# A hand-made order for the first batch, and TensorE in program order, in a kernel of attention and two feed-forward networks

## The chip, the cores and the metric

The kernel runs on one core of one Trainium2 chip. The metric is the device time of one execution, in microseconds (us); the median of three runs of the kernel before is 913.62 us. A core has five engines that run side by side: TensorE (PE) for matmuls, with its weight loads shown apart (PEld), VectorE (DVE), ScalarE (ACT), GpSimd (POOL), and SyncE (SP), which here issues nearly all DMA transfers. Each engine takes its instructions in a fixed order, made when the program is built, and they wait for one another by semaphores.

## The reference

```python
def _attn_ref(q, k, v):                       # (4, 8, 576, 64) each
    ...
    q_d = q.reshape(B, H, Sd, factor, D).mean(axis=3)      # pooled by 4: Sd = 144, also k_d, v_d
    out_up = np.repeat(sm_attn(q_d, k_d, v_d), factor, axis=2)
    mask = np.abs(pos[:, None] - pos[None, :]) < factor    # window of 7 keys
    ...
    return out_up + out_local
def _moe_ref(x, w1, w2, w3, w_out):            # 2304 tokens, 512 -> 768 -> 512
    h = np.maximum(np.maximum(x @ w1, x @ w2), x @ w3)
    return h @ w_out
def _moe2_ref(x, w_in, w_out):                 # 512 -> 2048 -> 512
    h = x @ w_in
    return np.maximum(0.01 * h, h) @ w_out
```

The attention's output, 4 batches of 576 rows with 8 heads of 64, is the 2304 x 512 input of the first network, whose output is that of the second.

## The kernel before, in words

**Tiling.** The 2304 tokens are eight *units* of 288, two to a batch (u = 0 to 7). For each unit the first network runs 18 groups L1 (six blocks m, three weights e) and four groups L2. A number is held as a high and a low part in a 22 bit format, so a product takes three matmuls: L1 is 12 matmuls of 128x128 by 288 columns, L2 is 18. The input parts are xh and xl, the hidden ones hh and hl. A group is called a *slot*: 22 slots a unit, `PU`. The second network (L3, L4) runs over chunks of 512 tokens when all units are done.

**Weights.** They arrive as 64 bit numbers. `split_weight` makes the two parts: two ScalarE instructions, two on VectorE (line 157 and 160), one on ScalarE, one subtraction on GpSimd or VectorE (line 166). The first network has 24 weight tiles (18 wA and 6 wO), named W1.

**Attention.** Pooled attention runs per batch and group of two heads (h = 0 to 3): load, pooling sums of q and k (line 478), scores on TensorE (492), softmax, transposes (516), product with v (531), result `up`. The windowed attention of batch 0 (u = 0 and 1) runs on TensorE: a band mask is added by a matmul (376), then scores (379), exponentials, transposes (417), product (426), and the sum with `up` gives x, xh and xl. That of batches 1 to 3 (units 2 to 7), the *local attention*, runs on the other engines with 128 rows of partitions: products of q and k on GpSimd (line 247), sums on VectorE (257) or ScalarE (260), softmax, products with v and sums on VectorE (291, 298) into O. `emit_T` then transposes O (nine transposes, line 573), adds `up`, and makes xh (ScalarE, 601) and xl (VectorE, 602) of the unit.

**What sets the order.** Only SP's order is that of the program (`manual_schedule(engines={SP})`). For the other four a scheduler with a model of the instructions' times picks the order, out of the order in which the program is written. There, the steps of batch 0's four heads come first, one step apart (`items`), with the weight conversions between them; then unit 0's slots, with the pieces for u = 1 in the first nine (`U1`), pieces of the local attention spread over each unit's slots (`loc_p`), the pooled steps of the later batches at given slots (`acts`), and `emit_T(u + 1)` in the second L2 slot. `keep_warm` puts 20 and 40 matmuls without use on TensorE. SBUF tiles of the first batch (`late_tile`) lie in the places of the last 12 weight tiles.

Of the kernel before, what the change touches and what calls it, by code (L numbers as in the profile page):

```python
# [23 lines left out]
G = 32  # L24
# [19 lines left out]
U1 = 9  # L44
AHEAD = 14
NA = 8
NWARM = (20, 40)
# [5 lines left out]
def local_global_attention_moe_kernel(  # L53
# [61 lines left out]
    ps_mm = p1.enter_context(tc.tile_pool(name="ps_mm", bufs=4, space=PSUM))  # L115
    ps_at = p1.enter_context(tc.tile_pool(name="ps_at", bufs=2, space=PSUM))

    ps_early = tc.alloc_tile_pool(name="ps_early", bufs=2, space=PSUM)
# [4 lines left out]
    for edge in (None, "first", "last"):  # L123
        bd = sup.tile([QB, KB], BF16, name=f"band_{edge}")
        P.memset(bd, 0.0)
        conds = [(1, -1, 0), (-1, 1, KB - QB)]
        if edge == "first":
            conds.append((1, 0, -(FAC - 1)))
        if edge == "last":
            conds.append((-1, 0, KB - FAC))  # L130
        for step, cm, base in conds:
            P.affine_select(
                out=bd, in_=bd, pattern=[[step, KB]], base=base, channel_multiplier=cm,
                compare_op=ALU.is_ge, fill=-(2.0**33),
            )
        bands.append(bd)

# [10 lines left out]
    def split_weight(raw, stage, lo_engine):  # L148
# [7 lines left out]
        A.activation(out=l3, in_=low16, func=AF.Copy, scale=2.0**-13, bias=-0.5 + 2.0**-14)  # L156
        V.scalar_tensor_tensor(  # L157
# [184 lines left out]
    def pl_load(what, h):  # L342
# [25 lines left out]
    def pl_scores(u, h, hh):  # L368
        qr, kr = pl[h, "q"], pl[h, "k"]
        pst = ps_early.tile([QB, 512], F32, tag="early", name="ps_ls")  # L370
        ps = pst[:, : NBLK * KB].rearrange("p (n k) -> p n k", n=NBLK)
        st = pst[:, NBLK * KB :]
        rows = slice(64 * hh, 64 * hh + 64)
        for j in range(NBLK):
            band = bands[1 if u == 0 and j == 0 else 2 if u == 1 and j == NBLK - 1 else 0]
            T.matmul(out=ps[:, j], lhsT=ident_b, rhs=band, start=True, stop=False)
            s0 = u * NCOL + j * QB
            qs, ks = slice(s0, s0 + QB), slice(s0, s0 + KB)
            T.matmul(out=ps[:, j], lhsT=qr[rows, qs], rhs=kr[rows, ks], start=False, stop=True)  # L379
        nm = sup.tile([QB, NBLK], F32, tag="plnm", bufs=4, name="plnm")  # L380
        if hh == 0:
            pl[u, h, "sum"] = sup.tile([QB, 2, NBLK], F32, tag="plsm", bufs=4, name="plsm")
        sm = pl[u, h, "sum"][:, hh]
        V.tensor_reduce(out=st[:, :NBLK], in_=ps, axis=AX.X, op=ALU.max, negate=True)
        V.tensor_scalar(out=nm, in0=st[:, :NBLK], scalar1=SCALE, scalar2=None, op0=ALU.mult)
        if hh == 0:
            if u == 0:
                pl[u, h, "e"] = late_tile([QB, 2, NBLK, KB], "ple")
            else:
                pl[u, h, "e"] = sup.tile([QB, 2, NBLK, KB], F32, tag="ple", bufs=2, name="ple")  # L390
        e = pl[u, h, "e"][:, hh]
        for j in range(NBLK):
            A.activation(
                out=e[:, j], in_=ps[:, j], func=AF.Exp, scale=SCALE,
                bias=nm[:, j : j + 1], accum_out=sm[:, j : j + 1],
            )
        if hh == 1:
            e, sm = pl[u, h, "e"], pl.pop((u, h, "sum"))
            sp = st[:, NBLK : 3 * NBLK].rearrange("p (x n) -> p x n", x=2)
            V.tensor_scalar(out=sp, in0=sm, scalar1=1e-9, scalar2=None, op0=ALU.add)  # L400
            V.reciprocal(out=sm, in_=sp)
            for x in range(2):
                (P if u == 0 else V).tensor_tensor(
                    out=e[:, x], in0=e[:, x], in1=sm[:, x].unsqueeze(2).to_broadcast((QB, NBLK, KB)), op=ALU.mult
                )

    def pl_aT(u, h):
# [4 lines left out]
        for n, (j0, j1) in enumerate(((0, 2), (2, 3))):  # L412
            pool, tag = (ps_mm, "mm") if u == n == 0 else (ps_at, "at")
            pt = pool.tile([KB, j1 - j0, 2, QB], F32, tag=tag, name="ps_lt")
            for j in range(j0, j1):
                for hh in range(2):
                    T.transpose(out=pt[:, j - j0, hh], in_=pl[u, h, "e"][:, hh, j], identity=ident[:QB, :QB])
# [13 lines left out]
    def pl_x(u, h):  # L431
# [38 lines left out]
    def ds_pool_qk(b, h):  # L470
# [478 lines left out]
```

## Time and profile before

| | us |
|---|---|
| median of three runs | 913.62 (913.1 to 914.03) |
| the profiled execution | 914.8, its span 913.0 |
| TensorE, weight loads busy | 860.4 and 754.7 |
| VectorE, ScalarE, GpSimd busy | 526.8, 412.8, 247.7 |
| mean granted TensorE clock | 0.932 of full speed |

The page shows the span in 40 slices: TensorE is 90% busy or more from the middle of the span on, and the clock is down in the first tenth and, now and then, up to 0.45 of it. All of GpSimd's work and most of VectorE's lies in the first 0.55 of the span. Durations overlap a little: an instruction can start before the one ahead of it on its engine has ended, so a sum of means is somewhat above the time that a row of them takes. The row of a matmul with fp32 operands counts two records for one matmul.

### The profile page before, as it was taken

Reading aid. Unit: us, or ns where it says so; the run is one execution under the profiler, and the core shown is the slowest. Engines: PE = TensorE matmul, PEld = TensorE weight load, DVE = VectorE, ACT = ScalarE, POOL = GpSimd, SP = SyncE. Lnnn points to the kernel's source line nnn. Section 1 sums busy time; section 2 is a strip of 40 time slices with the busy share of each in tenths; the row PEclk is TensorE's granted clock in tenths of the full one; section 3 lists DMA queues with packets and bytes.
Section 4 is the critical chain, followed back from the end, with each engine's and each line's share of the span. In section 5 each row is a group of like instructions: output and inputs, shape, how many; then the busy total and the mean of one; then the engine's idle time right before and its main releaser. Section 6 shows DMA issues by size and latency. Waiting matters only on the chain.

```text
span 913.0 us, 13518 instructions
## 1 busy us (share of the span) xinstructions
PE 860.4 (94%) x4912; PEld 754.7 (83%) x4914; DVE 526.8 (58%) x919; ACT 412.8 (45%) x1537; POOL 247.7 (27%) x195
## 2 busy tenths in 40 slices
PE   8799988997989989799999999999999999999995
PEld 4478888996978979699999888888887888788894
DVE  3587888887968696777475699242223322322321
ACT  2664754655647456572274687232223222222221
POOL 3553539764755566350111000000000000000000
PEclk9555979897999999799999999999999999999998
DMA  8700624442423133112062920020003000200000
GB/s 219 269 1 24 254 72 147 167 135 70 136 95 122 33 122 111 48 46 73 1 235 105 355 120 1 0 93 1 1 0 93 1 1 2 68 1 1 19 29 23
DMA packets 30132, 75.13 MB, mean 82 GB/s; under 512 B 3267, under 2 KB 8691, under 8 KB 30067
## 3 DMA queue, kind: packets, MB, share of 16 engines
q1 hardware_dynamic: 25459, 69.56, 22.8%
q10 hardware_dynamic: 4608, 4.72, 1.5%
q8 instruction: 38, 0.62, 0.3%
q14 instruction: 27, 0.22, 0.1%
HBM read 64.83 MB, written 9.44 MB: 81 GB/s over the span
## 4 chain that ended last, share of the span: by engine, by line
PE 74%; DVE 12%; DMA 7%; issue 2%; ACT 2%; SPq 1%; POOL 1%; ACTq 0%; POOLq 0%; DVEq 0%
PE ps_h L614 21%; PE acc L717 20%; PE ps_g L693 20%; PE ps_o L644 5%; DMA raw<-x2d 2%; PE ps_up L531 2%; DVE O L298 2%; DVE xl L602 2%; DMA wA<-in_wa_dram 2%; PE ps_ls L379 2%; PE ps_lo L426 1%; DMA sv<-in_vW_dram 1%; DVE wl L157 1%; DVE wy L160 1%; DVE x L594 1%
## 5 line engine op out<-in xcount | busy, mean ns | idle before, releaser
L614 PE MATMUL ps_h<-xh,wA 128*128 128x288 f32 x1152 | 204.5, 311 | 6.3 <-ACT xh L601 3.1
L614 PEld LDWEIGHTS ps_h<-xh,wA 128*128 128x128 f32 x1152 | 177.9, 201 | 9.2 <-ACT xh L601 3.3
L717 PE MATMUL acc<-w2o,gh 128*128 128x512 f32 x576 | 178.2, 391 | 0.9 <-ACT gh L704 0.9
L693 PE MATMUL ps_g<-x2h,w2i 128*128 128x512 f32 (+1 forms) x640 | 158.9, 370 | 0.0
L701 DVE TENSOR_TENSOR g<-g,ps_g 128x512 f32<-128x512 f32 (+1 forms) x80 | 50.7, 634 | 184.0 <-ACT g L700 183.9
L693 PEld LDWEIGHTS ps_g<-x2h,w2i 128*128 128x128 f32 x640 | 114.6, 188 | 22.9
L700 ACT ACTIVATE g<-ps_g 128x512 f32<-128x512 f32 (+1 forms) x80 | 44.3, 553 | 185.2 <-PE ps_g L693 185.1
L614 PE MATMUL ps_h<-xl,wA 128*128 128x288 f32 x576 | 116.5, 308 | 10.7 <-DVE xl L602 10.7
L717 PEld LDWEIGHTS acc<-w2o,gh 128*128 128x128 f32 x576 | 106.8, 188 | 23.7 <-ACT gh L704 1.8
L247 POOL TENSOR_TENSOR qkprod<-lq,lk 128x1344 f32<-128x1344 f32 x36 | 112.0, 3120 | 42.6 <-DVE O L298 25.6
L717 PE MATMUL acc<-w2o,gl 128*128 128x512 f32 x288 | 112.2, 391 | 0.1
L614 PEld LDWEIGHTS ps_h<-xl,wA 128*128 128x128 f32 x576 | 93.2, 199 | 12.9 <-DVE xl L602 11.9
L260 ACT ACTIVATE qkprod<-qkprod 128x64 f32<-128x64 f32 x364 | 87.6, 245 | 24.2 <-POOL qkprod L247 23.8
L693 PE MATMUL ps_g<-x2l,w2i 128*128 128x512 f32 (+1 forms) x320 | 79.6, 370 | 0.0
L644 PE MATMUL ps_o<-hh,wO 128*128 128x288 f32 x384 | 77.4, 298 | 0.0
L705 DVE TENSOR_TENSOR gl<-g,gh 128x512 fp32r<-128x512 f32 (+1 forms) x80 | 51.0, 638 | 39.6 <-ACT gh L704 35.1
L260 ACT ACTIVATION_READ_ACCUMULATOR qkprod<-qkprod 128x1 f32 x364 | 69.6, 191 | 0.0
L704 ACT ACTIVATE gh<-g 128x512 fp32r<-128x512 f32 (+1 forms) x80 | 47.1, 588 | 42.6 <-DVE g L701 42.2
L693 PEld LDWEIGHTS ps_g<-x2l,w2i 128*128 128x128 f32 x320 | 56.8, 188 | 10.9
L635 POOL TENSOR_TENSOR hl<-hm,hh 128x288 fp32r<-128x288 f32 x48 | 40.9, 854 | 88.3 <-ACT hh L634 84.7
L717 PEld LDWEIGHTS acc<-w2o,gl 128*128 128x128 f32 x288 | 54.1, 188 | 12.6 <-DVE gl L705 0.9
L631 DVE TENSOR_TENSOR hm<-hm,ps_h 128x288 f32<-128x288 f32 x96 | 42.3, 445 | 32.8 <-PE ps_h L614 26.9
(124 smaller groups left out, 1216.2 us busy)
## 6 DMA issues: line engine op xcount, KB each, us to landing
wA<-in_wa_dram SPq DMA_DIRECT2D x18, 512.0 KB
w2i<-in_w_in_dram SPq DMA_DIRECT2D x16, 512.0 KB
w2o<-in_w_out_dram SPq DMA_DIRECT2D x16, 512.0 KB
lv<-in_vL_dram SPq DMA_DIRECT2D x12, 480.0 KB
lk<-in_k_dram SPq DMA_DIRECT2D x11, 480.0 KB
dsrawv<-in_vP_dram SPq DMA_DIRECT2D x16, 288.0 KB
x2d<-ev ACTq DMA_DIRECT2D x32, 144.0 KB
raw<-x2d SPq DMA_DIRECT2D x16, 256.0 KB
```

The costliest lines, as they stand in the source:

```text
L247: P.tensor_tensor(out=pr, in0=in0, in1=in1, op=ALU.mult)
L260: A.activation(out=pr[:, r, j], in_=pr[:, r, j], func=AF.Copy, accum_out=sc[:, r, j : j + 1])
L614: T.matmul(out=ps, lhsT=wA[m, e][wi][:, kk * 128 : kk * 128 + 128], rhs=xx[:, kk] if u < PEU else xx[:, :, kk, :], start=n == 0, stop=n == ...
L631: V.tensor_tensor(out=t, in0=t, in1=ps, op=ALU.max)
L635: P.tensor_tensor(out=hl[:, m], in0=t, in1=hh[:, m].bitcast(F32), op=ALU.subtract)
L644: T.matmul(out=ps, lhsT=wO[m][wi][:, os_], rhs=xx[:, m], start=n == 0, stop=n == 3 * M1 - 1)
L693: T.matmul(out=ps, lhsT=w2i[m][wi][:, kk * 128 : kk * 128 + 128], rhs=xx[:, kk, :n], start=j == 0, stop=j == 3 * KC - 1,)
L700: A.activation(out=g, in_=ps, func=AF.Copy, scale=0.01)
L701: V.tensor_tensor(out=g, in0=g, in1=ps, op=ALU.max)
L704: A.activation(out=gh, in_=g, func=AF.Copy)
L705: V.tensor_tensor(out=gl, in0=g, in1=gh.bitcast(F32), op=ALU.subtract)
L717: T.matmul(out=accs[c, t], lhsT=a[:, ts], rhs=w, start=m == 0 and j == 0, stop=m == M2 - 1 and j == 2)
```

## The change

**Orders.** Batch 0 is written in the order of a table, `ORDER`: a letter is a step, a digit the head (or, for x y z u, the weight tile: the four steps of a conversion). In this part all five engines take the program's order. From unit 0 on, SP and TensorE do; the other three are scheduled as before. The pieces of u = 1 move to slots 3h, 3h + 4 and 3h + 5; the local attention begins at slot 15 (`U1`) and its pieces are spread to end at the slots in `DONE`; `emit_T` stands at the slots in `TURN`, and the steps of pooled attention at `DS0` plus `DSOFF`. Eight weight tiles are converted in the first part, the other 16 in unit 0's first 15 slots.

**Warm-up.** `fill` puts 20 matmuls at the start, 8 ahead of step O0, and one or two ahead of the steps B, C, O, M, N and P of each head.

**Engines.** GpSimd takes the pooling of q and k for batches 1 to 3 (two adds in place of a sum of VectorE), xl in `emit_T`, and the normalisation for u = 1. In W1's conversion one intermediate (`wl`) lies in PSUM, and GpSimd does all the low parts. The band mask is added for three blocks in one matmul. PSUM has one pool of seven banks for the first part. O has two buffers.

**Loads.** The tiles of v are padded with zero rows: 102 to 112 partitions and 72 to 80.

```diff
-U1 = 9
-AHEAD = 14
+U1 = 15
-NWARM = (20, 40)
+ORDER = (
+    "C0 A0 A1 L0 B0 D0 A2 C1 E0 L1 F0 B1 H0 G0 D1 I0 x0 C2 J0 L2 F1 E1 y0 K0 G1 D2 O0 L3 H1 E2 J1 M0 "
...
+FILL = {"B": 1, "C": 1, "O": 2, "M": 2, "N": 2, "P": 2}
+FILL0 = 20
+FILL1 = 8
+DONE = {2: 39, 3: 59, 4: 79, 5: 100, 6: 121, 7: 142}
+TURN = {2: 41, 3: 62, 4: 82, 5: 103, 6: 124, 7: 145}
+DS0 = {1: (15, 18, 21, 24), 2: (27, 38, 49, 60), 3: (68, 79, 90, 101)}
+DSOFF = {1: (0, 2, 5, 8, 6, 7, 11, 13), 2: (0, 5, 6, 9, 10, 11, 16, 20), 3: (0, 5, 6, 9, 10, 11, 16, 20)}
...
+    def fill(what, t, n=None):
+        for _ in range(FILL[what] if n is None else n):
+            T.matmul(out=t, lhsT=warm[:, :128], rhs=warm, start=True, stop=True)
...
-        l3 = stage.tile([128, 512], I32, tag="wy", bufs=4, name="wl3")
+        l3 = (stage.tile([128, 512], I32, tag="wy", bufs=4, name="wl3") if ps is None else ps()).bitcast(I32)
...
+    def pl_C(u, h):
...
+        if u == 0:
+            fill("C", pst[0])
+        for t in pst:
+            T.matmul(
+                out=t[:QB, :n], lhsT=ident_b, rhs=bands[u].rearrange("p n k -> p (n k)"), start=True, stop=False
+            )
         for j in range(NBLK):
...
+            for hh in range(2):
+                rows = slice(64 * hh, 64 * hh + 64)
+                T.matmul(
+                    out=pst[hh][:QB, j * KB : j * KB + KB], lhsT=qr[rows, qs], rhs=kr[rows, ks],
+                    start=False, stop=j == NBLK - 1,
+                )
...
-            V.tensor_reduce(out=t[:, j], in_=dst.pop((b, h, w)), axis=AX.X, op=ALU.add)
+            if b == 0:
+                V.tensor_reduce(out=t[:, j], in_=raw, axis=AX.X, op=ALU.add)
+            else:
+                P.tensor_tensor(out=raw[:, :, 0:2], in0=raw[:, :, 0:2], in1=raw[:, :, 2:4], op=ALU.add)
+                P.tensor_tensor(out=t[:, j], in0=raw[:, :, 0], in1=raw[:, :, 1], op=ALU.add)
...
-            V.tensor_tensor(
+            P.tensor_tensor(
                 out=xl[:, g0:g1].rearrange("p r a g -> p (r a g)"), in0=x32f, in1=xhf.bitcast(F32), op=ALU.subtract
             )
...
-    with tc.manual_schedule(engines={mybir.EngineType.SP}):
+    with tc.manual_schedule(engines={ET.SP, ET.PE, ET.DVE, ET.Activation, ET.Pool}):
...
+        for w in ORDER.split():
+            n = int(w[1])
+            if w[0] in "xyzu":
+                conv_step(W1[n])
+            elif w[0] == "L":
+                pl_pool_v(n)
+            else:
+                if w == "O0":
+                    fill("", scratch(0, "", "warm_ps"), FILL1)
+                steps[w[0]](0, n)
...
+    with tc.manual_schedule(engines={ET.SP, ET.PE}):
...
+        for u in range(PEU, NU):
+            at(TURN[u], lambda u=u: emit_T(u))
```

How the instructions stand on TensorE at the first scores of batch 0, before (`ps_sc` are the pooled scores, `ps_ls` the windowed ones of the two halves, `warm` the matmuls without use):

```order
L784 MATMUL warm_ps_212<-warm_210 128x512
L492 MATMUL ps_sc_237<-dsqke_233 72x144 x2
L492 MATMUL ps_sc_247<-dsqke_233 72x144 x2
L376 LDWEIGHTS ident_b_94
L376 MATMUL ps_ls_260<-band_first_122,ident_b_94 96x102
...
L379 MATMUL ps_ls_260<-skr_148,sqr_146 96x102
L376 LDWEIGHTS ident_b_94
L376 MATMUL ps_ls_260<-band_None_114,ident_b_94 96x102
```

and now:

```order
L166 MATMUL ps_ls_220<-warm_130 128x512
L421 LDWEIGHTS ident_b_94
L421 MATMUL ps_ls_220<-band0_108,ident_b_94 96x306
...
L421 MATMUL ps_ls_221<-band0_108,ident_b_94 96x306
L429 MATMUL ps_ls_220<-skr_137,sqr_135 96x102
L429 MATMUL ps_ls_221<-skr_137,sqr_135 96x102
...
L166 MATMUL ps_sc_240<-warm_130 128x512
L577 MATMUL ps_sc_240<-dsqke_231 72x144
L577 MATMUL ps_sc_241<-dsqke_231 72x144
```

The windowed scores now come ahead of the pooled ones, the band is loaded once for each half, the halves alternate, and each step begins with a matmul without use.

GpSimd's order at the end of unit 1, before (`hl` of the hidden part, `qkprod` the local products, `dse` the normalisation of pooled attention, `dsrawv` and `dsv32` the pooling of v; `hl_2320` is unit 2's):

```order
L635 TENSOR_TENSOR hl_1716<-hm_2126,hh_1715 128x288
L509 TENSOR_TENSOR dse_1856<-dse_1856,dssum_1857 72x576
L247 TENSOR_TENSOR qkprod_2418<-lq_2028,lk_2030 128x1344
L467 TENSOR_TENSOR dsv32_2372<-dsrawv_2327 72x256
L466 TENSOR_TENSOR dsrawv_2379<-dsrawv_2379 72x4x128
L247 TENSOR_TENSOR qkprod_2521<-lq_2346,lk_2348 128x1344
L467 TENSOR_TENSOR dsv32_2415<-dsrawv_2379 72x256
```

and now, with the pooling of q and k (`dsraw`, `dsqk`) and unit 2's xl:

```order
L550 TENSOR_TENSOR dsv32_2450<-dsrawv_2366 72x256
L566 TENSOR_TENSOR dsqk_2640<-dsraw_2510 128x144
L759 TENSOR_TENSOR hl_1613<-hm_2170,hh_1612 128x288
L291 TENSOR_TENSOR qkprod_2662<-lq_2514,lk_2516 128x1344
L566 TENSOR_TENSOR dsqk_2640<-dsraw_2512 128x144
L618 TENSOR_TENSOR dse_2141<-dse_2141,dssum_2142 72x576
L549 TENSOR_TENSOR dsrawv_2660<-dsrawv_2660 72x4x128
L291 TENSOR_TENSOR qkprod_2790<-lq_2514,lk_2516 128x1344
L726 TENSOR_TENSOR xl_2242<-x32_2253,xh_2241 128x512
L726 TENSOR_TENSOR xl_2242<-x32_2260,xh_2241 128x512
L726 TENSOR_TENSOR xl_2242<-x32_2265,xh_2241 128x128
```

Unit 2's xl, which stood on VectorE, comes on GpSimd behind the 17th local product; the two rows of `qkprod` ahead of it belong to a later unit.

## Rows read from the trace of the kernel before

**Rows 1.** Busy time by stage: stretch, length, busy (count), clock, DMA, GB/s.

```profile
core 0: us, PE busy (x) PEld busy (x) DVE busy (x) ACT busy (x) POOL busy (x), PEclk, DMA share, GB/s
0.00:40.00 40.00, 31.54 (x135) 16.88 (x137) 17.75 (x46) 16.38 (x59) 19.96 (x41) 0.81 0.86 263
40.00:60.00 20.00, 18.01 (x76) 12.42 (x75) 14.21 (x38) 13.80 (x53) 10.49 (x10) 0.50 0.09 31
60.00:90.00 30.00, 30.00 (x134) 25.97 (x133) 23.18 (x42) 16.43 (x49) 12.61 (x11) 0.50 0.06 18
90.50:161.70 71.20, 62.64 (x429) 58.81 (x428) 61.09 (x111) 42.65 (x155) 45.78 (x30) 0.88 0.44 158
...
216.00:425.00 209.00, 189.40 (x1372) 184.80 (x1372) 163.84 (x280) 120.22 (x739) 111.72 (x68) 0.94 0.28 89
...
504.20:913.00 408.80, 397.91 (x1824) 328.31 (x1823) 155.46 (x251) 140.37 (x252) 0.00 (x0) 0.99 0.13 44
```

**Rows 2.** Timeline of TensorE, batch 0's scores: start, length, what, idle before.

```profile
8.35 0.72 PE L492 MATMUL ps_sc<-dsqke 64*72 64x144 f32 x8
...
11.77 0.41 PE L379 MATMUL ps_ls<-skr,sqr 64*96 64x102 f32 x2
...
21.12 1.23 PE L492 MATMUL ps_sc<-dsqke 64*72 64x144 f32 x8 [3.01 <-DVE plnm L385]
...
26.70 0.65 PE L379 MATMUL ps_ls<-skr,sqr 64*96 64x102 f32 x2
```

**Rows 3.** Timeline of TensorE: warm-up matmuls, and the other steps at both clocks.

```profile
12.34 5.78 PE L784 MATMUL warm_ps<-warm 128*128 128x512 bf16 x26 [0.16 <-issue]
...
31.36 3.19 PE L784 MATMUL warm_ps<-warm 128*128 128x512 bf16 x7 [0.22 <-issue]
...
60.23 2.18 PE L531 MATMUL ps_up<-dsvaT 72*128 72x144 f32 x8
...
63.01 1.01 PE L417 MATMUL ps_lt<-ident,ple 96*102 96x96 f32 x5
...
78.31 2.49 PE L426 MATMUL ps_lo<-plt,sv 102*128 102x96 f32 x10
...
101.29 1.48 PE L426 MATMUL ps_lo<-plt,sv 102*128 102x96 f32 x12
...
118.54 0.70 PE L417 MATMUL ps_lt<-ident,ple 96*102 96x96 f32 x6
...
131.38 0.58 PE L426 MATMUL ps_lo<-plt,sv 102*128 102x96 f32 x4
...
157.28 1.56 PE L531 MATMUL ps_up<-aT,dsv 72*128 72x144 f32 x8 [0.25 <-ACT aT L524]
...
201.40 0.66 PE L516 MATMUL ps_aT<-ident,dse 72*72 72x72 f32 x8
```

**Rows 4.** The chain that ended last, in unit 7: start, length, what.

```profile
465.79 28.80 PE ps_h L614 x216
```

**Rows 5.** Groups on GpSimd: busy us, mean ns; idle before, its releasers.

```profile
L247 POOL TENSOR_TENSOR qkprod<-lq,lk 128x1344 f32<-128x1344 f32 x36 | 112.0, 3120 | 42.6 <-DVE O L298 25.6 <-ACT qkprod L260 12.0 <-issue 4.6
L635 POOL TENSOR_TENSOR hl<-hm,hh 128x288 fp32r<-128x288 f32 x48 | 40.9, 854 | 88.3 <-ACT hh L634 84.7 <-DVE dssum L504 3.4
...
L466 POOL TENSOR_TENSOR dsrawv<-dsrawv 72x512 f32<-72x512 f32 x12 | 15.4, 1283 | 34.4 <-DMA dsrawv<-in_vP_dram 34.4
L509 POOL TENSOR_TENSOR dse<-dse,dssum 72x576 f32<-72x576 f32 x12 | 13.7, 1144 | 5.0 <-DVE dssum L504 4.5 <-DVE lp L279 0.5
L448 POOL TENSOR_TENSOR xl<-x,xh 128x288 fp32r<-128x288 f32 x8 | 9.0, 1122 | 18.2 <-ACT xh L447 18.2
L467 POOL TENSOR_TENSOR dsv<-dsrawv 72x256 f32<-72x256 f32 x12 | 8.8, 731 | 8.2 <-PE ps_up L531 7.9
```

**Rows 6.** Timeline of GpSimd: its first local products.

```profile
137.79 9.18 POOL L247 TENSOR_TENSOR qkprod<-lq,lk 128x1344 f32<-128x1344 f32 x3
```

**Rows 7.** Groups by line: unit's xl on VectorE, unit's transposes on TensorE.

```profile
L602 DVE TENSOR_TENSOR xl<-x,xh 128x512 fp32r<-128x512 f32 (+3 forms) x18 | 19.9, 1116 | 4.5 <-ACT xh L601 4.5
...
L573 PE MATMUL ps_x<-ident,O 128*128 128x128 f32 x54 | 9.9, 298 | 0.5 <-DVE x L594 0.5
```

More of the change, by code (lines that the diff above doesn't have):

```diff
@@ L383, in pl_scores @@
[L383 to L404, printed above, removed]
-                )
@@ new lines, in pl_H, with pl_I @@
+    def pl_H(u, h):
+        st, sm = pl.pop((u, h, "st")), pl[u, h, "sum"]
+        pl.pop((u, h, "ps"))
+        for hh in range(2):
+            sp = st[hh][:, NBLK : 2 * NBLK]
+            V.tensor_scalar(out=sp, in0=sm[:, hh], scalar1=1e-9, scalar2=None, op0=ALU.add)
+            V.reciprocal(out=sm[:, hh], in_=sp)
+    def pl_I(u, h):
+        e, sm = pl[u, h, "e"], pl.pop((u, h, "sum"))
+        P.tensor_tensor(out=e, in0=e, in1=sm.unsqueeze(3).to_broadcast((QB, 2, NBLK, KB)), op=ALU.mult)
@@ new lines, in pl_O @@
+    def pl_O(u, h):
+        pts = []
+        for n, (j0, j1) in enumerate(((0, 2), (2, 3))):
+            pt = scratch(u, "at", "ps_lt")
+            if u == n == 0:
+                fill("O", pt)
+            pt = pt[:KB, : (j1 - j0) * 2 * QB].rearrange("p (j h q) -> p j h q", h=2, q=QB)
+            for j in range(j0, j1):
+                for hh in range(2):
+                    T.transpose(out=pt[:, j - j0, hh], in_=pl[u, h, "e"][:, hh, j], identity=ident[:QB, :QB])
+            pts.append(pt)
+        pl[u, h, "pt"] = pts
@@ L408, in pl_aT, with pl_o @@
+    def pl_o(u, h):
         if u == 0:
@@ L502, in ds_scores @@
-        sm, sp = sm[:, 2 * hh : 2 * hh + 2], pst[:, 2 * SD + 2 : 2 * SD + 4]
-        V.tensor_scalar(out=sp, in0=sm, scalar1=1e-9, scalar2=float(FAC), op0=ALU.add, op1=ALU.mult)
-        V.reciprocal(out=sm, in_=sp)
+        pst = dst[b, h, "ps"] = [scratch(b, "at", "ps_sc") for hh in range(2)]
+        if b == 0:
+            fill("B", pst[0])
+        for c in range(2):
+            for hh in range(2):
+                rows = slice(64 * hh, 64 * hh + 64)
+                T.matmul(
+                    out=pst[hh][:QC, c * SD : c * SD + SD], lhsT=t[rows, 0, c * QC : c * QC + QC],
+                    rhs=t[rows, 1, :], start=True, stop=True,
+                )
@@ new lines, in ds_G @@
+    def ds_G(b, h):
+        pst, nm = dst[b, h, "ps"], dst.pop((b, h, "nm"))
+        if b:
+            dst[b, h, "e"] = small(b, [QC, 2, 2, SD], "dse")
+        e4 = dst[b, h, "e"]
+        sum4 = dst[b, h, "sum"] = pools[b].tile([QC, 4], F32, tag="dssum", bufs=2, name="dssum")
+        for hh in range(2):
+            for c in range(2):
+                A.activation(
+                    out=e4[:, hh, c, :], in_=pst[hh][:QC, c * SD : c * SD + SD], func=AF.Exp, scale=SCALE / 16.0,
+                    bias=nm[:, hh, c : c + 1], accum_out=sum4[:, 2 * hh + c : 2 * hh + c + 1],
+                )
@@ L506, in ds_norm, with ds_J @@
+    def ds_J(b, h):
+        st, sum4 = dst.pop((b, h, "st")), dst[b, h, "sum"]
+        dst.pop((b, h, "ps"))
+        for hh in range(2):
+            sm = sum4[:, 2 * hh : 2 * hh + 2]
+            V.tensor_scalar(out=st[hh][:, 2:4], in0=sm, scalar1=1e-9, scalar2=float(FAC), op0=ALU.add, op1=ALU.mult)
+            V.reciprocal(out=sm, in_=st[hh][:, 2:4])
     def ds_norm(b, h):
@@ L535, in ds_pv, with ds_v @@
                 )
+    def ds_v(b, h):
+        ps = dst.pop((b, h, "up"))
         if h == 0:
@@ L779, in local_global_attention_moe_kernel @@
-        V.memset(warm, 0.0)
-        warm_ps = ps_mm.tile([128, 512], F32, tag="mm", name="warm_ps")
-        def keep_warm(n):
-            for _ in range(n):
-                T.matmul(out=warm_ps, lhsT=warm[:, :128], rhs=warm, start=True, stop=True)
-        keep_warm(NWARM[0])
-        for i, (_, _, f) in enumerate(items):
-            f()
-            while ci < min(li, AHEAD * (i - 9) // (len(items) - 10)):
-                conv_w1(W1[ci])
-                ci += 1
-        keep_warm(NWARM[1])
```

365 lines of the change are left out of this document (193 added, 172 removed), and 3 rows, old and new, of the table ORDER.

## The prediction

> **What bounds the kernel now.** I read the busy time by stages first, with the granted TensorE clock in its last columns [rows 1]. The reader is to see four stages. In the first 90 us the first batch's attention runs before any layer can start; TensorE idles 8.5 of the first 40 us, and from 40 to 90 us its clock is at 0.50, the lower level of 1.2 GHz. From 60 to 90 us it is busy 30.00 of 30 us and stays at that level. From 90.5 to 161.7 us unit 0 runs. From 216 to 425 us four units of the first network run beside the local attention: 209 us, in which TensorE is busy 189.4 at clock 0.94, VectorE 163.8 (78%), ScalarE 120.2, GpSimd 111.7 (53%). From 504.2 us the second network runs to the end, 408.8 us with TensorE busy 397.9.
>
> Then the chain of waits gave the pace of undisturbed layers [rows 4]: 216 matmuls in 28.80 us, 0.133 us each. A unit has 18 x 12 + 4 x 18 = 288 of them, 38.4 us, so one of its 22 slots takes 1.745 us. The four units took 209 / 4 = 52.3 us each. Their own matmuls, two pooled heads and nine transposes each need about 46 us, so 6.3 us per unit is waiting and low clock. VectorE's xl, 1.116 us in the mean over 18 pieces [rows 7], sits between the transposes and the layer.
>
> The second network is left as it is and only its TensorE order is now that of the program, which already alternates the two layers as the trace does. I carry its 408.8 us over unchanged. So the change is worth what it does before 504.2 us.
>
> **The change part by part.** I follow TensorE, because it now runs in program order and everything has to meet it.
>
> *First batch.* Per head the trace shows the same six steps at both levels of the clock [rows 2, 3]. Windowed scores, from the end of the pooled scores to the last score: 11.77 + 0.41 - (8.35 + 0.72) = 3.1 us at the upper level, 26.70 + 0.65 - (21.12 + 1.23) = 5.0 at the lower. Pooled scores 0.72 and 1.23. Pooled transposes 0.66 for eight, and twice that at the lower level, 1.3. Windowed transposes 0.70 for six, against 1.01 for five, so 1.2. Pooled product 1.56 and 2.18. Windowed product 1.48 for its twelve records, against 2.49 for ten, so 3.0. A head is 8.2 or 13.9 us, four heads 32.8 or 55.6. The new scores load the band in two matmuls instead of six; no row shows those, so I price them as the six. The change adds 8 warm-up matmuls before O0 and 10 per head, 48 in all, at 5.78 / 26 = 0.222 or 3.19 / 7 = 0.456 us: 10.7 or 21.9 us. The first block of 20 replaces 25 that ended at 8.35, which I keep. That is 51.9 us at the upper level and 85.9 at the lower, before waiting. TensorE idled 8.5 us in the first 40 us [rows 1], and with program order it waits for each step of the other engines, so I keep these 8.5: 60 or 94 us.
>
> Which of the two is the question of this stage. The row from 60 to 90 us has no warm-up matmul, the row from 0 to 40 us has 58 of them among the same steps, and its mean clock is 0.81 at 79% busy. The new stage mixes 68 of them in, nearest to that row: (32.8 + 10.7) / 0.81 = 53.7, which with 8.35 and 8.5 makes 70.6. I take 65, between that and full clock, since the band matmuls are fewer. Here a rule speaks the other way from a row. The Trainium skill, "TensorE: Matmul & The Clock Gate", section "What's actually happening", says that a TensorE kept busy is let up to the full clock and that idleness takes it back. The trace disagrees in one stretch: fully busy with small matmuls from 60 to 90 us, it stayed at 0.50. By the rule this stage would be 60 us, by that row 94.
>
> The other engines' work in this stage is smaller than TensorE's: in the first 90 us VectorE was busy 55, ScalarE 47, GpSimd 43 [rows 1], with twelve weight conversions where now there are eight, and with more than half of the second half-batch (u = 1), which now moves into unit 0. The padded loads only make data land sooner; the heads' q and k go in the same order, so I give that nothing. If they came late, the 8.5 us would grow.
>
> *Unit 0, slots 0 to 14.* 15 x 1.745 = 26.2 us, and the u = 1 attention between them at 3.1 + 0.70 + 1.48 = 5.3 us per head, 21.1 for four: 47.3, taken as 48. Sixteen conversions and the exponentials lie beside it. Before, unit 0 took 71 us [rows 1] with 61 us of VectorE beside 62.6 of TensorE, so this cover is not thick: I allow 60 as the upper end. Slot 15 starts at 65 + 48 = 113 us.
>
> *The local attention up to unit 2.* Before, the first local product on GpSimd started at 137.79 us, 5.8 us after the last u = 1 product (131.38 + 0.58) [rows 3, 6]. Now a slot of layer work follows that product, which leaves 4 us after slot 15: 117 us. From there GpSimd's queue decides, and this is where the change adds a wait. Unit 2's xl moves to GpSimd, and in its queue stand ahead of it, from the first pooling add on, 17 local products, 14 + 14 pooling adds (seven heads, though unit 2 needs four), 7 + 6 adds for v, 5 normalisations, 7 hl and one weight part, as the order shows. With the durations of [rows 5]: 17 x 3.120 = 53.0; a 128x288 pooling add as hl, 0.854, the half-size one 0.43, together 18.0; 7 x 1.283 + 6 x 0.731 = 13.4; 5 x 1.144 = 5.7; 7 x 0.854 = 6.0; the weight part about 1.4. The xl itself, four times a 128x288 piece of at most 1.122, is 3 to 4.5. That is 101 us, less some 0.04 us of overlap for each of 74 instructions: 97. The pooling adds are not in the trace on GpSimd; bounds from the nearest rows, 0.72 (72x512 in 1.283, by elements) and 1.122, move this by -3 and +6 us. TensorE in the same slots 15 to 43 needs 50.6 us of layers, four heads at 0.72 + 0.66 + 1.56 = 2.94 and nine transposes at about 1.65 (a sixth of 9.9 [rows 7]): 64. So TensorE waits some 33 us for GpSimd in this stretch, the hl of unit 1 and its second layer queued behind the same products. Unit 2 starts with its xl at 117 + 97 = 214 us, hardly before the 216 of now [rows 1].
>
> *After that.* VectorE has lost the xl and the q and k pooling, and GpSimd's queue is one unit ahead, since 17 of 36 local products are done. From slot 44 TensorE needs 132 x 1.745 = 230.3 us, seven pooled heads 20.6 and five sets of transposes 5 x 1.65 = 8.3: 259. Of the 6.3 us per unit that four units lose now I keep half, 13 us: a GpSimd queue with 3 us products ahead of hl will still make the second layer wait. Bounds 0 and 25.
>
> *Sum.* 65 + 48 + 4 + 97 + 259 + 13 = 486 us for the start of the second network, against 504.2. With 408.8 and the 1.8 us by which the profiled execution (914.8) exceeds its span, 896.6. The median of the runs is 1.2 us below that execution, so 895.
>
> **The rivals.** *GpSimd does not hold unit 2.* For it: GpSimd was busy only 53% in the steady units [rows 1], and its products wait for VectorE [rows 5]. Against it: its order is fixed and its durations are measured. Then TensorE runs from slot 15 at its own pace: 161 x 1.745 = 281, twelve heads 35.3, six transposes 9.9, 13 of waits, 339 us. 65 + 48 + 339 = 452, and the end is 861.
>
> *The first batch stays at the lower clock (the slower side).* One mechanism: small matmuls in the first batch do not lift the clock, and the 48 warm-up matmuls spread among them cost 21.9 us instead of helping. For it: 60 to 90 us at 0.50 while fully busy. Against it: the 0 to 40 us row. The stage then ends at 94 us and the kernel at 895 + 29 = 924. It decides from a stage end of 65 + 18 = 83 us; above that the kernel is slower. By the skill's rule above this rival would not happen.
>
> *The units do not get faster.* TensorE in program order stands at each late step where the old order went around it, and from unit 2 on the pace is that of now, 504.2 - 216 = 288 us. 65 + 48 + 4 + 97 + 288 = 502, end 911: the saved start is given back.
>
> **How the numbers follow.** Forecast 0.58, with its own range 879 to 909. GpSimd not holding, 0.14, at 861. Lower clock, 0.16, at 924, of which a small part lies under the present time. Units no faster, 0.12, around 911, split on both sides. A measurement of this kernel can tell about 0.2% from no change, so faster means below 911.8: 0.57 + 0.14 + 0.06 + 0.02 = 0.79. Within 0.2%: 0.06. Slower: 0.15. The range from 864 to 917 leaves out the lower part of the second case and the upper part of the third.
>
> **What would show it.** Right: the first layer matmul between 55 and 75 us with the clock mostly up before it, the first local product near 117 us, GpSimd nearly without idle from there until unit 2's xl, and TensorE waiting for that xl or for hl. Then units 3 to 5 near 46 us. Wrong: TensorE's first layer after 83 us at clock 0.50; GpSimd idle while TensorE waits; or a second network that does not take 409 us.

## The result, and the profile after

The changed kernel takes 926.87 us (925.69 to 927.9) against 913.83 us for the kernel before, run beside it; the ratio is 1.0142, with a 95% interval of 1.0124 to 1.016. The forecast was 895 us, so it went the other way. The profiled execution took 927.9 us, its span is 926.1 and its mean clock 0.946, higher than before at a longer time.

Busy time by stages of the changed kernel, columns as in [rows 1]:

```profile
0.00:40.00 40.00, 31.41 (x208) 19.07 (x212) 26.48 (x78) 21.10 (x90) 23.35 (x41) 0.87 0.95 285
40.00:60.00 20.00, 13.20 (x100) 10.85 (x101) 14.37 (x35) 16.50 (x39) 12.24 (x11) 0.86 0.57 219
...
102.20:212.30 110.10, 69.22 (x460) 64.57 (x460) 88.93 (x129) 51.45 (x323) 90.91 (x71) 0.80 0.39 127
214.40:517.60 303.20, 269.85 (x1952) 262.84 (x1951) 175.10 (x300) 142.55 (x716) 131.31 (x108) 0.94 0.20 69
517.60:926.10 408.50, 398.03 (x1826) 328.49 (x1824) 155.47 (x251) 140.37 (x252) 0.00 (x0) 0.99 0.14 50
```

The stage bounds come from the timeline (start, length, what). On TensorE, the first layer matmul and the first of unit 2:

```profile
58.65 0.61 PE L738 MATMUL ps_h<-xh,wA 128*128 128x288 f32 x1
...
214.37 0.29 PE L738 MATMUL ps_h<-xh,wA 128*128 128x288 f32 x1
```

On GpSimd, the first local product and unit 2's xl:

```profile
102.10 3.06 POOL L291 TENSOR_TENSOR qkprod<-lq,lk 128x1344 f32<-128x1344 f32 x1
...
209.31 2.94 POOL L726 TENSOR_TENSOR xl<-x,xh 128x512 fp32r<-128x512 f32 x3
```

The reader is to see three things. The first batch ends 31.9 us earlier (58.65 against the 90.5 of [rows 1]). At unit 2 that is used up: 214.4 against 216. And from unit 2 to the second network it takes 303.2 us, where it took 504.2 - 216 = 288.2. The second network is as long as it was.

**Where VectorE stood.** In the stretch from 102 to 212 us VectorE was busy 88.9 of 110 us. Its costliest group there is one of the smallest instructions of the local attention, the minimum with the window mask, 21 columns wide (line, operation, tiles, shapes, count; busy us, mean ns; idle before):

```profile
L310 DVE TENSOR_TENSOR ls<-ls,mask 128x21 f32<-128x21 f32 x6 | 22.9, 3816 | 1.7 <-ACT qkprod L304 1.7
L335 DVE TENSOR_TENSOR pvprod<-lp,lv 128x1344 f32<-128x1344 f32 x12 | 18.6, 1546 | 0.0
```

All twelve of them after (min, median and max in ns; first and last start):

```profile
L310 DVE TENSOR_TENSOR ls<-ls,mask x12: 171/1008/7662, 106.8 to 358.0; 128x21 f32<-128x21 f32 x12
```

and before:

```profile
L266 DVE TENSOR_TENSOR ls<-ls,mask x12: 165/281/2384, 144.6 to 408.9; 128x21 f32<-128x21 f32 x12
```

The shortest takes 0.17 us, the longest 7.66; added up they take 30.0 us, against 8.3 before. The timeline of VectorE at one of them:

```profile
119.62 1.54 DVE L342 TENSOR_REDUCE O<-pvprod 128x192 f32<-128x1344 f32 x1
121.08 7.53 DVE L310 TENSOR_TENSOR ls<-ls,mask 128x21 f32<-128x21 f32 x1
128.54 0.81 DVE L591 TENSOR_REDUCE ps_sc<-ps_sc 72x2 f32<-72x288 f32 x2
```

and that of GpSimd beside it:

```profile
118.34 3.10 POOL L291 TENSOR_TENSOR qkprod<-lq,lk 128x1344 f32<-128x1344 f32 x1
121.38 0.87 POOL L566 TENSOR_TENSOR dsqk<-dsraw 128x144 f32<-128x144 f32 x2
122.18 0.69 POOL L565 TENSOR_TENSOR dsraw<-dsraw 128x288 f32<-128x288 f32 x1
122.81 0.76 POOL L550 TENSOR_TENSOR dsv<-dsrawv 72x256 f32<-72x256 f32 x1
123.50 3.07 POOL L291 TENSOR_TENSOR qkprod<-lq,lk 128x1344 f32<-128x1344 f32 x1
126.51 0.84 POOL L566 TENSOR_TENSOR dsqk<-dsraw 128x144 f32<-128x144 f32 x2
127.30 1.28 POOL L549 TENSOR_TENSOR dsrawv<-dsrawv 72x512 f32<-72x512 f32 x1
```

The minimum ends at 128.61 us, 0.04 us after the last of a run of GpSimd instructions without a pause (127.30 + 1.28 = 128.58). Eight of the twelve took over 0.5 us, and each of those ends 0.04 us after a GpSimd instruction. It is recorded as work, so neither the busy share nor the waits show it as waiting. Both its operands lie in SBUF. The product beside it, `pvprod`, which has one operand in PSUM, took its usual 1.546 us in the mean. The Trainium skill, "SBUF — State Buffer", section "Who interferes with whom", says that a VectorE instruction with two inputs in SBUF contends with a GpSimd instruction that reads SBUF, and one with a single such input doesn't; these rows agree, and experiment e1 tests it.

**Where TensorE stood.** Its waits from 214.4 to 517.7 us (what waited, for whom; us in total, times, longest):

```profile
PE ps_o L768 <- POOL hl L759: 8.5, 3, 4.1
PE ps_o L768 <- ACT hh L758: 7.2, 3, 5.2
PE ps_aT L629 <- POOL dse L618: 5.9, 1, 5.9
PE ps_sc L577 <- ACT up L666: 5.3, 2, 3.7
PE ps_x L697 <- DVE x L718: 2.2, 3, 0.9
PE ps_up L651 <- DVE dssum L613: 1.8, 1, 1.8
```

That is 15.7 us ahead of second layers, 13.0 ahead of pooled steps, and with smaller ones 33.4 in all, which is 303.2 less the busy 269.85. What such a wait rests on is seen in the chain of waits in unit 4:

```profile
371.02 1.46 DVE pvprod L335
372.48 0.36 DVE hm L755
...
374.21 1.56 DVE pvprod L335
375.77 1.46 DVE O L342
377.24 0.37 DVE hm L755
377.63 0.45 ACT hh L758
378.12 0.85 PE ps_o L768 x2
```

and on TensorE:

```profile
378.12 0.85 PE L768 MATMUL ps_o<-hh,wO 128*128 128x288 f32 x2 [5.23 <-ACT hh L758]
```

TensorE waits 5.2 us in its second layer, for a maximum (`hm`) that VectorE takes behind products of the local attention, and cannot go on to anything else.

### The profile page after: what moved, and what is told of

Read it like the earlier page. It is cut to its first block, busy times and chain, and to the rows that moved or that the text cites. A ratio compares the mean times of both kernels' runs of the same rounds, so it can differ in the third digit from the quotient of the medians.

```text
span 926.1 us, 13553 instructions
## 1 busy us (share of the span) xinstructions
PE 825.3 (89%) x4886; PEld 727.6 (79%) x4890; DVE 497.6 (54%) x880; ACT 410.7 (44%) x1537; POOL 293.6 (32%) x263
## 4 chain that ended last, share of the span: by engine, by line
PE 62%; DVE 13%; POOL 6%; DMA 6%; ACT 6%; issue 4%; SPq 1%; DVEq 0%; ACTq 0%; POOLq 0%
PE acc L841 20%; PE ps_g L817 20%; PE ps_h L738 13%; PE ps_o L768 6%; POOL qkprod L291 4%; DVE ls L310 3%; ACT qkprod L304 2%; DMA raw<-x2d 2%; DVE pvprod L335 2%; DVE O L342 2%; DMA dsrawv<-in_vP_dram 2%; DMA wA<-in_wa_dram 1%; DVE ls L301 1%; PE ps_up L651 1%; DVE x L718 1%
## 5 line engine op out<-in xcount | busy, mean ns | idle before, releaser
L738 PEld LDWEIGHTS ps_h<-xh,wA 128*128 128x128 f32 x1152 | 173.6, 195 | 4.1 <-issue 2.5
L817 PEld LDWEIGHTS ps_g<-x2h,w2i 128*128 128x128 f32 x640 | 114.5, 188 | 22.9
L738 PE MATMUL ps_h<-xl,wA 128*128 128x288 f32 x576 | 112.8, 304 | 0.0
L768 PE MATMUL ps_o<-hh,wO 128*128 128x288 f32 x384 | 86.3, 320 | 13.1 <-ACT hh L758 13.1
L304 ACT ACTIVATE qkprod<-qkprod 128x64 f32<-128x64 f32 x364 | 87.5, 245 | 22.9 <-POOL qkprod L291 22.7
L768 PEld LDWEIGHTS ps_o<-hh,wO 128*128 128x128 f32 x384 | 68.6, 209 | 14.2 <-ACT hh L758 14.0
L768 PE MATMUL ps_o<-hl,wO 128*128 128x288 f32 x192 | 61.5, 320 | 16.8 <-POOL hl L759 16.7
L759 POOL TENSOR_TENSOR hl<-hm,hh 128x288 fp32r<-128x288 f32 x48 | 42.2, 878 | 102.1 <-ACT hh L758 101.9
```

What stands on the lines that cost most here:

```text
L304: A.activation(out=pr[:, r, j], in_=pr[:, r, j], func=AF.Copy, accum_out=sc[:, r, j : j + 1])
L738: T.matmul(out=ps, lhsT=wA[m, e][wi][:, kk * 128 : kk * 128 + 128], rhs=xx[:, kk] if u < PEU else xx[:, :, kk, :], start=n == 0, stop=n == ...
L759: P.tensor_tensor(out=hl[:, m], in0=t, in1=hh[:, m].bitcast(F32), op=ALU.subtract)
L768: T.matmul(out=ps, lhsT=wO[m][wi][:, os_], rhs=xx[:, m], start=n == 0, stop=n == 3 * M1 - 1)
L817: T.matmul(out=ps, lhsT=w2i[m][wi][:, kk * 128 : kk * 128 + 128], rhs=xx[:, kk, :n], start=j == 0, stop=j == 3 * KC - 1,)
```

## The experiments

Two theories were held against the rival that GpSimd's own work is the bound (C): VectorE stands behind GpSimd through the minima (A), and TensorE loses the time by its fixed order from unit 0 on (B). Each kernel ran beside the kernel before; the table goes by the ratio to it, and a difference of ratios times 914 us is a difference of times.

| run | what differs from the changed kernel | ratio, 95% interval | unit 2 starts | second network starts | 12 minima, us |
|---|---|---|---|---|---|
| changed | | 1.0142 (1.0124 to 1.016) | 214.4 | 517.6 | 30.0 |
| e1 | mask in PSUM | 0.9876 (0.9854 to 0.9899) | 190.8 | 494.2 | 2.1 |
| e2 | TensorE free | 0.9676 (0.9635 to 0.9717) | 191.8 | 472.1 | 22.8 |
| e3 | pooling on VectorE | 1.0081 (1.0054 to 1.0108) | 212.0 | 509.2 | 15.5 |
| e4 | xl on VectorE | 1.0155 (1.0109 to 1.0202) | 214.5 | 522.6 | 29.5 |
| e5 | e1 + e2 | 0.9453 (0.9436 to 0.9469) | 187.5 | 456.2 | 2.0 |
| e6 | e1 + e2 + e3 | 0.9421 (0.9402 to 0.9441) | 179.0 | 454.8 | 2.0 |
| e7 | no warm-up within the batch | 1.0174 (1.0129 to 1.022) | 217.7 | 524.9 | 31.8 |
| e8 | pooled steps wider apart | 1.011 (1.0076 to 1.0144) | 210.1 | 518.4 | 29.2 |
| e9 | before, mask in PSUM | 0.9998 (0.9977 to 1.002) | 213.8 | 503.4 | 2.0 |
| e10 | e2 + e3 + e4 | 0.9523 (0.9474 to 0.9571) | 179.5 | 462.9 | 14.7 |
| e11 | TensorE free from unit 2 | 0.9712 (0.968 to 0.9745) | 212.4 | 475.9 | 35.7 |
| e12 | e1 + e2 + e3 + e4 | 0.9462 (0.9433 to 0.9491) | 177.9 | 453.9 | 2.0 |

**e1, the mask's operand in PSUM.**

```diff
-        V.tensor_tensor(out=sl, in0=sl, in1=masks[half], op=ALU.min)
...
+        A.activation(out=(mk := pb[:, n + 2 * RU :]...), in_=masks[half], func=AF.Copy)
+        V.tensor_tensor(out=sl, in0=sl, in1=mk, op=ALU.min)
```

> Edit: ScalarE copies the 21 columns of the window mask into the PSUM tile lp, and VectorE's minimum (line 310) reads one operand in SBUF and one in PSUM, instead of two in SBUF. Everything else is as changed. In the changed kernel these 12 small minima were recorded as 30.0 us of VectorE, each ending 0.04 us after the end of a GpSimd instruction. Theory A (VectorE stands behind back-to-back GpSimd work through these minima): the 12 minima fall to about 2 us, unit 2's xl ends 15 to 25 us before the 212 us of the changed kernel, the time falls to 900 to 915. Theory B (the fixed order of TensorE from unit 0 on loses the time): the minima may get short, the time stays within 4 us of 926.9. Theory C (GpSimd's longer queue, by its own work, holds unit 2): unit 2's xl still ends near 212 us, time 922 to 927.

Measured: 904.28 us (902.22 to 905.25), within what A gave. The minima (their operand in PSUM goes by the name of its tile, lp):

```profile
L312 DVE TENSOR_TENSOR ls<-ls,lp x12: 153/172/179, 104.2 to 332.4; 128x21 f32<-128x21 f32 x12
```

The stretch up to unit 2's xl, and the one from unit 2 to the second network, columns as in [rows 1]:

```profile
102.20:190.50 88.30, 65.29 (x462) 61.89 (x463) 70.00 (x129) 52.29 (x327) 83.62 (x68) 0.86 0.43 136
190.80:494.20 303.40, 271.80 (x1952) 265.27 (x1950) 168.47 (x300) 145.56 (x735) 137.93 (x112) 0.94 0.22 73
```

No minimum is above 0.18 us, and unit 2 starts 23.6 us earlier; 2.4 of these are a first batch that ended at 56.28 us in this run, which the edit does not touch. From unit 2 on nothing changes: 303.4 against 303.2 us. So A holds for the first stretch only.

**e9, the same edit on the kernel before.**

> Edit of e1 on the kernel before: the mask's second operand in PSUM. There the 12 minima took 8.3 us in all, three of them over 1 us. If the price of a minimum is set by how dense GpSimd's work stands (theory A), there is little to get here: 0 to 5 us below the kernel before. If the edit itself gives the 22.6 us of e1 (by another order of the scheduled engines, not by the operand), 15 us or more.

Measured: no difference (ratio 0.9998), though its minima fell from 8.3 to 2.0 us. So the edit by itself is worth nothing where GpSimd is less dense. It also lets the scheduler order VectorE, ScalarE and GpSimd otherwise, and in the changed kernel that was not held apart from the operand. But four pairs of kernels differ in this edit alone, and the gain goes with the time that the twelve minima lose:

| pair | minima lose, us | ratio falls by |
|---|---|---|
| changed, e1 | 27.9 | 0.0266 |
| e2, e5 | 20.8 | 0.0223 |
| e10, e12 | 12.7 | 0.0061 |
| before, e9 | 6.3 | 0.0002 |

The first two falls are clear of the intervals, the last two not.

**e2, TensorE's order free from unit 0 on.**

```diff
-    with tc.manual_schedule(engines={ET.SP, ET.PE}):
+    with tc.manual_schedule(engines={ET.SP}):
```

> Edit: from unit 0 on only SP takes the program's order; TensorE's order is picked by the scheduler again, as in the kernel before. Theory A (minima behind GpSimd): the wait remains, the time stays within 6 us of 926.9. Theory B (fixed order of TensorE): the 72 us of gaps of TensorE between 100 and 518 us fall to about 35, the time falls to 885 to 900. Theory C (GpSimd's queue): unit 2's xl still near 212 us, a gain of at most 10 us.

Measured: 883.65 us (882.93 to 889.72), just below what B gave. TensorE's idle time between 100 and 518 us, the gaps of B, fell from 74 to 32 us. But unit 2 also came 22.6 us earlier (3.4 of it from a first batch that ended at 55.24), which B had not said, and the minima still took 22.8 us.

**e11, TensorE's order free from unit 2 on** (the manual order is left at `u == 2`).

> Edit on the changed kernel: TensorE in program order only up to the end of unit 1, then picked by the scheduler. e2, with a free TensorE from unit 0 on, starts unit 2 at 191.8 us against 214.4, and then takes 280.5 us against 303.3 to the second network. If the two halves are separate: unit 2 at 210 to 216 us and then 278 to 285 us, time 900 to 907. If all is lost in the first two units and carried on: 920 to 927. If what e2 gains after unit 2 was only its earlier local work: 912 to 920.

Measured: 888.83 us, a larger gain than any of the three gave. The stretch from unit 2 to the second network:

```profile
212.40:475.90 263.50, 259.71 (x1951) 253.68 (x1950) 179.52 (x300) 140.91 (x716) 128.28 (x108) 1.00 0.24 80
```

and all of TensorE's waits in it:

```profile
PE ps_h L738 <- DVE hm L755: 1.2, 1, 1.2
PE ps_h L738 <- ACT hm L752: 1.2, 1, 1.2
PE ps_h L738 <- ACT ev L771: 1.0, 1, 1.0
```

Unit 2 starts as late as in the changed kernel, and then 263.5 us do what took 303.2: TensorE idles 3.8 us instead of 33.4, and its clock is 1.00 instead of 0.94, which is the other 10.1 us (busy 259.71 instead of 269.85). These 40 us are the price of the fixed order after unit 2, and no wait of more than 1.2 us is left.

Two things limit this reading. With TensorE free the scheduler also orders the other engines anew: in unit 4 the last `hl` ended 8.6 us after the last matmul that it rests on in the changed kernel, and 3.1 us after it in e11, where VectorE took the maximum behind one product:

```profile
345.59 0.44 DVE L755 TENSOR_TENSOR hm<-hm,ps_h 128x288 f32<-128x288 f32 x1
```

How much of the 40 us comes from that order, and how much from TensorE going around late steps, was not held apart. And e11 starts unit 2 late. In e2, where it starts 20.6 us earlier, the same stretch takes

```profile
191.80:472.10 280.30, 270.97 (x1957) 264.10 (x1958) 190.12 (x315) 151.96 (x801) 145.18 (x118) 0.95 0.25 82
```

and all but 3.8 us of the lead is gone at the second network (472.1 against 475.9 us); the two ratios, 0.9676 and 0.9712, cannot be told apart. So the gains of a free order before and after unit 2 do not add.

**e5, both edits.**

> Edits of e1 and e2 together: the mask's second operand in PSUM, and TensorE's order from unit 0 on picked by the scheduler. If the minima and the fixed order are two causes that add: 926.9 - 22.6 - 43.2 = 861. If they overlap because both end in the same wait for unit 2 (TensorE waits 18 us between 165 and 192 us in e2): 868 to 880. If the fixed order was the only cause and the minima cost only what it made of them: 881 to 886.

Measured: 866.11 us (865.98 to 866.95). In ratios, the mask is worth 0.0266 with the fixed order and 0.0223 with the free one; the free order 0.0466 with the mask in SBUF and 0.0423 with it in PSUM. So each edit keeps most of its worth beside the other. The time lies between what adding (861 us) and overlapping (868 to 880) gave, and the 0.0043 (4 us) by which the two fall short of adding are no more than the intervals allow by chance.

**e3 and e4, the work moved to GpSimd taken back.**

```diff
-            if b == 0:
+            if True:
                 V.tensor_reduce(out=t[:, j], in_=raw, axis=AX.X, op=ALU.add)
```
```diff
-            P.tensor_tensor(
+            V.tensor_tensor(
                 out=xl[:, g0:g1]..., in0=x32f, in1=xhf.bitcast(F32), op=ALU.subtract
```

> Edit: the pooling of q and k for batches 1 to 3 goes back to one sum of VectorE each (24 sums); GpSimd loses 48 adds. Theory A: GpSimd is less dense, so the minima wait less (30.0 us to some 15), VectorE gains that and pays 24 sums at 0.743 us (17.8 us): about even, 920 to 928. Theory B: no change within 4 us. Theory C (GpSimd's queue): the 14.9 us that 27 of these adds take ahead of unit 2's xl go, which ends near 198 us, time 910 to 916.

> Edit: xl of units 2 to 7 goes back to VectorE. Theory A: six more groups of two-operand SBUF work stand behind GpSimd on VectorE; the 18 pieces take 1.1 us or more each (20 us in the kernel before) and the time rises by 3 to 10 us. Theory B: no change within 4 us. Theory C (GpSimd's queue): xl no longer waits for GpSimd's order, unit 2 starts some 5 us earlier, time 918 to 924.

Measured: e3 923.86 us (919.73 to 926.33), the minima at 15.5 us and the time as A gave, unit 2 at 212.0, where C wanted its xl at 198. C falls as the cause. e4 930.44 (924.12 to 933.07): by the ratios no difference can be told.

**e10, e6 and e12: what the move to GpSimd is worth once TensorE is free.**

> Edits of e2, e3 and e4 together: TensorE's order from unit 0 on picked by the scheduler, xl and the pooling of q and k on VectorE again; what is left of the change is the first batch's order, its warm-up, the early local attention and the loads. If the hand-made first part carries the gain: 875 to 895, near e2's 883.7. If the move to GpSimd carries part of it once TensorE is free: 895 to 910.

> As e5, and the pooling of q and k for batches 1 to 3 back on VectorE. If GpSimd's queue then holds unit 2 (theory C, once the two other causes are gone): 5 to 12 us below e5. If VectorE is the nearer bound: 3 to 10 us above e5 (ten of the 24 sums at 0.743 us, 7.4 us, fall ahead of unit 2's xl). Within 3 us of e5: neither.

> e6 (mask in PSUM, free TensorE, pooling on VectorE) with xl of units 2 to 7 on VectorE too. xl reads two operands in SBUF, so by theory A it stands behind GpSimd: its pieces take 1 us or more in the mean instead of 0.5, and the time is 2 to 8 us above e6's 863.5. If the order of GpSimd's queue matters more: 1 to 5 us below.

Measured: e10 872.4, e6 863.52, e12 865.6 us. e10 lies below both of its ranges. With the mask in SBUF, xl and pooling on GpSimd make the kernel slower by 0.0153 (e10 to e2, 14 us of 914); with the mask in PSUM the same move makes -0.0009 (e12 to e5), which is nothing. So no price of the move is left where the minima do not wait. e6 is the best version, 5.8% faster than the kernel before (863.13 to 865.93), but the medians of e5, e6 and e12 lie within 0.3% and their intervals touch: pooling on one engine or the other cannot be told apart there. Of e12's two-operand xl pieces on VectorE, one took 4.05 us and the median piece 0.67: the mechanism is there, but the mean of 0.88 us is below the 1 us expected, and the 2 us above e6 are the least of the expected range.

**e8, the pooled steps spread wider, TensorE in program order.**

```diff
-DS0 = {1: (15, 18, 21, 24), ...
-DSOFF = {1: (0, 2, 5, 8, 6, 7, 11, 13), 2: (0, 5, 6, 9, 10, 11, 16, 20), ...
+DS0 = {1: (15, 19, 23, 27), ...
+DSOFF = {1: (0, 2, 5, 8, 6, 9, 12, 13), 2: (0, 5, 6, 9, 10, 13, 17, 20), ...
```

> Edit on the changed kernel, TensorE still in program order: the heads of batch 1's pooled attention begin 4 slots apart instead of 3, and the transposes and products of all batches stand 1 to 2 slots further behind the scores. If the fixed order costs time because each pooled step is written too close behind the one before it: the 28 us of TensorE's gaps ahead of pooled steps fall to 15 or less and the time falls by 8 to 20 us. If a fixed order loses the time wherever the steps stand (the other engines' own order decides when they come): within 5 us of 926.9.

Measured: 927.05 us. The waits moved and did not go: from 100 to 518 us TensorE's idle time is 71.4 us, where it was 74.2. Ahead of pooled steps it fell from 35.7 (the expectation had 28) to 27.9 us, not to 15. The two largest waits are:

```profile
PE ps_o L768 <- POOL hl L759: 22.0, 5, 8.3
PE ps_sc L577 <- ACT up L666: 9.9, 4, 5.6
```

So this one wider placing gains nothing that can be told. Others, and a second layer written later, were not tried.

**e7, without the warm-up inside the first batch** (`FILL` and `FILL1` at 0).

> Edit on the changed kernel: the 48 warm-up matmuls spread over the first batch are left out, the 20 at the start stay. If they hold the clock up (the mean clock was 0.87 in the first 40 us and 0.86 from 40 to 60 us): the first layer, which began at 58.7 us, begins at 70 to 85 us with clock near 0.5 to 0.6, and the time rises by 8 to 25 us. If they only cost their own time (48 at 0.222 us, 10.7 us): the first layer begins at 48 to 54 us and the time falls by 3 to 10 us. If the first batch waits for other engines and neither matters: 55 to 62 us and within 4 us of 926.9.

Measured: 933.47 us (926.78 to 936.03), not to be told from the changed kernel. The stage itself can be read:

```profile
0.00:40.00 40.00, 30.93 (x172) 21.84 (x174) 26.00 (x77) 20.77 (x90) 23.34 (x41) 0.68 0.90 285
40.00:60.00 20.00, 14.57 (x77) 13.56 (x74) 12.64 (x32) 14.20 (x34) 9.72 (x9) 0.50 0.40 146
```

The clock is 0.68 and 0.50 where it was 0.87 and 0.86, and the first layer begins at 62.6 us. In the eleven kernels that have the same first part with the warm-up it began at 54.6 to 58.7. That is just above the range of the expectation in which they do not matter (55 to 62), and below the one in which they hold the clock up (70 to 85). So the 48 matmuls do hold the clock up and pay for themselves in this stage, but by some 4 to 8 us and not by the 34 that lay between the prediction's two cases.

## Why the prediction was wrong, step by step

**First batch: about the right time, by two errors.** Forecast 65 us, measured 58.65. The clock was up, so the row from 0 to 40 us was the right one to go by for it. The terms were off both ways. TensorE idled 8.6 us in the first 40 us, but 6.8 more up to 58.65; and its work was smaller. From the first scores on:

```profile
8.35:58.65 50.30, 36.10 (x282) 25.87 (x285) 36.96 (x106) 34.75 (x124) 29.88 (x28) 0.86 0.83 268
```

That is 36.1 us busy at a mean clock of 0.86, where the prediction had 43.5 at full clock, and 14.2 idle instead of 8.5. A good part of the work is the windowed scores, priced as in the old form at 3.1 us per head. With one band matmul for each half and the halves alternating they take 1.1:

```profile
73.66 0.43 PE L421 MATMUL ps_ls<-band,ident_b 96*96 96x306 bf16 x2
74.02 0.77 PE L429 MATMUL ps_ls<-skr,sqr 64*96 64x102 f32 x12
```

The second rival, the lower clock, did not come; its price was too high as well: in e7, where the clock was low, the stage ended at 62.6 us, and the prediction's prices without the 21.9 us of warm-up make 94 - 21.9 = 72.

**Slots 0 to 14: too long.** Forecast 48 us, measured 96.4 - 58.65 = 37.8. It is the same term: the windowed scores of three heads took 1.1 to 1.5 us each, those of the first head came before 58.65, and the prediction had four at 3.1.

**Unit 2's xl: the right time by two errors.** Forecast 214 us, its end measured at 212.25. The local attention started at 102.1 instead of 117, and the stretch took 110 us instead of 97. GpSimd's durations were well taken, as its groups in this stretch show (beside xl, 2.9 us):

```profile
L291 POOL TENSOR_TENSOR qkprod<-lq,lk 128x1344 f32<-128x1344 f32 x17 | 51.9, 3063 | 2.8 <-DVE dssum L613 1.8 <-DMA lk<-in_k_dram 1.0
L549 POOL TENSOR_TENSOR dsrawv<-dsrawv 72x512 f32<-72x512 f32 x7 | 9.0, 1286 | 7.7 <-DMA dsrawv<-in_vP_dram 7.7
L565 POOL TENSOR_TENSOR dsraw<-dsraw 128x288 f32<-128x288 f32 x13 | 8.7, 680 | 0.0
L618 POOL TENSOR_TENSOR dse<-dse,dssum 72x576 f32<-72x576 f32 x5 | 5.7, 1145 | 6.5 <-DVE dssum L613 6.5
L566 POOL TENSOR_TENSOR dsqk<-dsraw 128x144 f32<-128x144 f32 x13 | 5.7, 454 | 0.0
```

But GpSimd was not "nearly without idle": it was busy 90.9 of 110.1 us. Of the 19 us of idle time 8.3 ended with a step of VectorE, 8.7 with a load (v and k), the rest with ScalarE and TensorE. Behind most of it stand the minima: VectorE was held by GpSimd in six of them for 22.9 us, 3.7 of these after unit 2's xl was done. This term is missing in the sum. The row for it was in the trace of before, at 2.38 us for the longest and 8.3 in all, and the prediction did not use it. In e1 the minima are gone, GpSimd is busy 83.6 of 88.3 us, and the step's picture holds.

**After unit 2: the step that failed.** "Of the 6.3 us per unit that four units lose now I keep half, 13 us." It was 303.2 - 259 = 44 us: 33.4 of waits, and 10.9 of a lower clock (busy 269.85). That is 31 us more, nearly the whole miss of 32. The forecast took the loss from a kernel whose TensorE could go around a late step, and let it shrink because VectorE had less to do. With a fixed order each late step is waited for. Where the order is free from unit 2 on (e11, with the other engines' order set anew beside it), the loss is 263.5 - 259 = 4.5 us, below the forecast, and the time of 888.8 us lies below 895: the GpSimd queue that was to make the second layer wait cost almost nothing there. That holds for a unit 2 that starts late, with the other engines ahead: in e2 the loss is 280.3 - 259 = 21.3 us, within the prediction's bounds of 0 and 25. The last rival named the right mechanism, TensorE standing at late steps, but let it cost no more than the old pace (288 us), and gave it 0.12.

**Second network: right.** Forecast 408.8 us, measured 408.5.

**The change as a whole.** What is left of the change in e10, the hand-made first part with its loads, the early local attention, the new places of the later steps and the second buffer of O, takes 0.0477 off. The move of pooling and xl to GpSimd gives back 0.0153, and the fixed order of TensorE from unit 0 on another 0.0466: 1 - 0.0477 + 0.0153 + 0.0466 = 1.0142. These are steps from kernel to kernel in one order, so they add up by themselves; in another order they are worth something else (pooling taken back under the fixed order, e3, gives 0.0061). The parts of e10 were not tried by themselves. Why the scheduler puts local products on VectorE ahead of the maxima that a fixed TensorE needs next stays open.

## What to carry to other kernels

An order written by hand can pay where the work is a known chain, as in the first batch, which ended 31.9 us earlier here. Where four engines braid, fixing one engine turns each late step into a wait of that engine, so price it by every step it can no longer go around. Before moving work onto GpSimd, list the VectorE instructions with two operands in SBUF, small ones too, since their price rose here with how dense GpSimd became; one operand in PSUM took it away. And look at the longest instruction of a group, not only at its mean: 0.17 and 7.66 us in one row is a wait that is counted as work.

## What the runs showed of the hardware

A 128x21 minimum on VectorE with two SBUF operands took 0.17 us beside an idle GpSimd and up to 7.66 us beside a busy one, and it did not always get through after the GpSimd instruction that was running: from 121.08 us on nine of them ended before it did (the seven rows above, two of which hold two). At other places it came through at the first change of instruction, as from 106.78 to 108.18 us. None stood on over a pause of GpSimd: of the eight long ones four ended at a pause, and four at the end of a local product although the next instruction followed at once. What lets it through at those, and not at others, is open. With one operand in PSUM all twelve took 0.15 to 0.18 us beside the same GpSimd work.
